# Splitting k on all 128 partitions and moving it within SBUF, and one product on GpSimd, in an attention, MoE and MLP kernel

## The chip, the cores and the metric

The kernel runs on one core of a Trainium2 chip, in one launch. The metric is the device time of an execution in microseconds (us), where less is better. Three executions of the kernel before took 638.43, 638.69 and 638.76 us; the median is 638.69. One more execution was recorded by the profiler: it took 637.58 us, of which the span of recorded instructions is 635.9. All durations below come from that one.

## The reference

Three layers follow one another, all in fp32: windowed attention, a mixture of four experts in which every expert is applied to every token with a weight, and an MLP with a squared ReLU.

```python
def _attn_ref(q, k, v):                      # B, H, S, D = 2, 8, 576, 64
    scores = 1 / sqrt(D) * np.matmul(q, k.transpose(0, 1, 3, 2))
    rel = pos[:, None] - pos[None, :]
    bias = slopes[:, None, None] * (-np.abs(rel))[None]
    mask = (rel >= 0) & (rel < 128)
    scores = np.where(mask, scores + bias[None], -1e9)
    attn = np.exp(scores - scores.max(-1, keepdims=True))
    return np.matmul(attn / (attn.sum(-1, keepdims=True) + 1e-9), v)

def _moe_ref(x, domain_probs, w1, w2):       # N, D, E, F = 1152, 512, 4, 1024
    p = domain_probs / (domain_probs.sum(-1, keepdims=True) + 1e-9)
    for e in range(E):
        out += p[:, e:e + 1] * (np.maximum(x @ w1[e], 0.0) @ w2[e])

def _moe2_ref(x, w_in, w_out):               # 512 -> 2048 -> 512
    h = np.maximum(x @ w_in, 0.0)
    return h * h @ w_out
```

## The kernel before

TensorE multiplies in the number format fp32r, which holds fewer bits than fp32. So an operand is split in two: a high part, which is the value rounded to fp32r (`rounded`, lines L555 on ACT and L557 on DVE), and a low part, which is what the rounding left (`rest`, L561, on DVE or POOL). A product is then high by high, low by high and high by low.

The attention is cut into 20 units. A unit is two heads of one batch and some queries with the keys in their windows. Units 0 to 3 are the first query tile and take q and k unsplit. Units 4 to 11 hold 256 queries and 384 keys each, units 12 to 19 hold 192 queries and 320 keys. A unit of the later sixteen has these steps, named as in the code: `lq`, `lk`, `lv` load q (L699, two DMAs in units 12 to 19), k (L706) and v (L714; L719 and L720 too in units 12 to 19), all on SP's queue; `qh`, `kh` round q and k; `ql`, `kl` take the rests; the scores on PE (L922, L931); the join with the mask (L949) and the row maximum (L969) on DVE; the exponential on ACT (L979); the division by the row sum (`no`, L1002 on ACT or L1008 on POOL); the transpose of the probabilities on PE (`tp`, L1018); masks on POOL (L1039); the product with v on PE (`pv`, L812), whose result is again rounded (xh) and its rest taken (xl).

Scores need k in a tile `khl` of 128 partitions by 2 heads by keys: the high part of both heads on partitions 0 to 63, the low part on partitions 64 to 127. q is laid out twice over the partitions, so one matmul of 128 rows does two of the three products. The load of k puts both heads beside each other on 64 partitions (`rk`, 64x2x384 or 64x2x320), so `kh` and `kl` of a unit are one instruction each on 64 partitions with 768 or 640 columns.

While attention runs, PE also does the first items of the first expert: the first products (`hps`, L1103) and the second (`yacc`, L1343). A class `Plan` puts the steps of units and items in one order before anything is emitted. Each step states which engines can do it, how long it holds the engine and when its result is there (numbers written in the code), what it depends on, which buffer slots it takes (`SLOTS`) and a due time. The planner takes, again and again, the engine that can start soonest, and on it the step that is due first. The order in which steps are taken is the order of the instructions on each engine's queue, which runs strictly in order. So costs and due times in the code set the order, and what is late on the chip waits in that order.

The weights of the experts are multiplied by the router's probabilities of a token, divided by their sum: `norm_probs` does this on all 1152 tokens at once, on DVE (a sum L1086, a reciprocal L1087 and a product L1088 on the 128x9x4 tile `pt`). Its first reader is the evacuation of the first expert's output (L1359, `y<-yacc,pt`). The name `pt` is also that of the transposed attention probabilities, which are other tiles.

From 120 us on the kernel is experts and MLP alone, where the change touches nothing.

Of the kernel before, what the change touches and what calls it, by code (L numbers as in the profile page):

```python
# [8 lines left out]
F32 = mybir.dt.float32  # L9
F32R = mybir.dt.float32r  # L10
# [6 lines left out]
P = 128  # L17
# [31 lines left out]
class Plan:  # L49
# [21 lines left out]
    def add(  # L71
        self, name, opts, fn, deps=(), takes=(), bufs=(), due=0.0, follow=(), cold=True,
        shared=False
    ):
        t = dict(
            name=name, opts=opts, fn=fn, deps=[d for d in deps if d], takes=list(takes),
            bufs=list(takes) + list(bufs), due=due + LATER.get(name, 0.0), end=None, follow=[d for d in follow if d],
            cold=cold, shared=shared,
        )
        for b in t["bufs"]:  # L80
            b.users += 1
        self.tasks.append(t)
        return t
# [74 lines left out]
def kernel(  # L158
# [14 lines left out]
    nc = tc.nc  # L173
    B, H, _, S = qT.shape
    D = v.shape[2] // H
# [25 lines left out]
    pt = probs_sum[:, :, 0:E]  # L201
    psum_p = const.tile([P, NTILE], F32, name="psum_p")

    def f32(ap):
        return ap.bitcast(F32)
# [318 lines left out]
    def where(key, u, opts):  # L524
# [1 line left out]
        return [x for x in opts if x[0] == ENGINE.get((key, u), x[0])]  # L526

    SLOTS = dict(
        rq=3, rk=2, rv=4, qh=2, ql=2, khl=2, sc=2, rsc=2, tp=2, ts=5, st=5, pt=4, work=2, y=2, h=4
    )  # L530
    plan = Plan(SLOTS)
    actx = ExitStack()
    abias = actx.enter_context(tc.tile_pool(name="abias", bufs=1))
    asp = actx.enter_context(tc.tile_pool(name="asp", bufs=2))
    psum = dict(
        sc=[actx.enter_context(tc.tile_pool(name="psc", bufs=2, space=PSUM))],
# [13 lines left out]
    def a_tile(kind, shape, dtype):  # L550
        return asp.tile(shape, dtype, tag=kind, name=kind, bufs=SLOTS[kind])

    def rounded(eng, out, in_):
        if eng == "ACT":
            nc.scalar.activation(out=out, in_=in_, func=ACTF.Copy)  # L555
        else:
            nc.vector.tensor_copy(out=out, in_=in_)  # L557

    def rest(eng, out, in0, in1):
        e = nc.gpsimd if eng == "POOL" else nc.vector  # L560
        e.tensor_tensor(out=out, in0=in0, in1=f32(in1), op=ALU.subtract)  # L561


    def act(n):
        return ("ACT", 0.01 + 0.00098 * n, 0.11 + 0.00098 * n)

    def dve(n):
        return ("DVE", 0.07 + 0.00105 * n, 0.17 + 0.00105 * n)

    def gps(n):  # L570
        return ("POOL", 0.17 + 0.0021 * n, 0.24 + 0.0021 * n)
# [24 lines left out]

    bias = abias.tile([P, H, 2 * P], BF16, name="bias")

    rel = abias.tile([P, 2 * P], F32, name="rel")

    below = abias.tile([P, P], F32, name="below")

# [66 lines left out]
    task = {}  # L669
# [6 lines left out]
    def unit_tasks(u, due):  # L676
# [3 lines left out]
        G = 2 * nb  # L680
# [4 lines left out]


        raw = t0 == 0
        b_ = {k: Buf(k) for k in ("rq", "rk", "rv", "qh", "ql", "khl", "pt", "work")}
        prev = {"pv": task.get(("pv", u - 1)) or task.get(("pv", u - 2))}

        def add(key, opts, fn, **kw):
            task[key, u] = plan.add(f"{key}{u}", opts, fn, **kw)
            return task[key, u]
# [8 lines left out]
                )  # L702

        def load_k(eng):
            t = b_["rk"].tile = a_tile("rk", [D, G, nk], F32)
            nc.sync.dma_start(  # L706
                out=t, in_=kT[bs[0], 2 * c:2 * c + 2, :, k0:q1].rearrange("a p s -> p a s")
            )
# [25 lines left out]


        def kh(eng):
            b_["khl"].tile = a_tile("khl", [P, G, nk], F32R)
            rounded(eng, b_["khl"].tile[0:D], b_["rk"].tile)

        def kl(eng):  # L740
            t = b_["khl"].tile
            rest(eng, t[D:P], b_["rk"].tile, t[0:D])

        end = due[-1]
        first = due[0]
# [11 lines left out]
        if not raw:  # L757
            tqh = add("qh", [act(G * nq), dve(G * nq)], qh, shared=True, deps=[lq], takes=[b_["qh"]],
                      bufs=[b_["rq"]], due=first - 9.0)
            tkh = add("kh", [act(G * nk), dve(G * nk)], kh, shared=True, deps=[lk], takes=[b_["khl"]],  # L760
                      bufs=[b_["rk"]], due=first - 9.1)
            tql = add("ql", [gps(G * nq), dve(G * nq)], ql, shared=True, deps=[tqh], takes=[b_["ql"]],
                      bufs=[b_["rq"], b_["qh"]], due=first - 8.2)
            tkl = add("kl", [dve(G * nk), gps(G * nk)], kl, shared=True, deps=[tkh],
                      bufs=[b_["rk"], b_["khl"]], due=first - 8.3)

        split = []
        wide = 0
# [2 lines left out]
        pos = 0  # L771
        for i, t in enumerate(range(t0, t1)):
            split += job_tasks(
                u, i, t, add, b_, due[i], loads if raw else [tqh, tql, tkh, tkl], G, q0, k0,
                pos, wide,
            )
            pos += tile_n(t) * (1 if t == 0 else 2)
# [307 lines left out]
    def norm_probs(eng):  # L1085
        nc.vector.tensor_reduce(out=psum_p, in_=probs_sum, axis=mybir.AxisListType.X, op=ALU.add)  # L1086
        nc.vector.reciprocal(out=psum_p, in_=psum_p)  # L1087
        nc.vector.tensor_tensor(  # L1088
            out=pt, in0=pt, in1=psum_p.unsqueeze(2).to_broadcast([P, NTILE, E]), op=ALU.mult
        )  # L1090


    ytile = {}

# [882 lines left out]
    t_pt = plan.add("pt", [("SP", 0.6, 6.0)], lambda eng: nc.sync.dma_start(  # L1977
        out=pt, in_=probs.rearrange("(t p) e -> p t e", p=P)
    ), deps=[wtask["load", 3]], due=50.0)
    t_np = plan.add("np", [("DVE", 0.9, 1.0)], norm_probs, deps=[t_pt], due=60.0)  # L1980
    for i in parted[:PER - (RAW1 + RAW2) // FTQ]:
        weight_parts(i)
    after = [item_tasks(it) for it in range(FT)]
# [108 lines left out]
```

## Time and profile before

| | us |
|---|---|
| median of three executions | 638.69 |
| profiled execution | 637.58 |
| its span of instructions | 635.9 |
| PE busy in the span | 630.1 (99%) |
| DVE, ACT, POOL busy | 473.5, 301.5, 377.5 |

The span and 1.68 us around it make up the profiled execution. The median of the others lies 1.11 us above it. The granted TensorE clock is full (1.00, 2.4 GHz) in every slice after the start. A matmul's records overlap, since matmuls are pipelined: what one costs is the distance to the start of the next. On SP the records are the issues of DMAs: what one costs the queue is again the distance to the next start, and the data land later.

### The profile page before, as it was taken

To read this page: it belongs to the slowest core of one execution; us is meant where nothing else is said; L and a number is where in the kernel's file an instruction comes from. 1 tells how busy PE (TensorE), PEld (TensorE's weight loads), DVE (VectorE), ACT (ScalarE), POOL (GpSimd) and SP (SyncE) were. 2 spreads that over 40 slices of the span, in tenths; PEclk is the share of its full clock that TensorE was granted. 3 is DMA by queue.
4 is the path that set the end of the run, shared out by engine and by line. 5 is a ranking of instruction groups with operands and counts; after the bars stand their busy time and mean duration, and the time that the engine had idled before them with its cause. 6 is when DMAs were issued, how large, how long until landed. Compare 5 with 4: busy or idle time off the path is not lost.

```text
span 635.9 us, 11035 instructions
## 1 busy us (share of the span) xinstructions
PE 630.1 (99%) x3918; PEld 565.0 (89%) x3918; DVE 473.5 (74%) x1027; ACT 301.5 (47%) x769; POOL 377.5 (59%) x487
## 2 busy tenths in 40 slices
PE   9999999999999999999999999999999999999997
PEld 7788889899998998998998998999999898998996
DVE  7899876388887777777777777668768767667463
ACT  8889866145444344334334444354554544343220
POOL 3597853089676446446447546246687776766531
PEclk9999999999999999999999999999999999999999
DMA  8953430222134434434434433311123223001012
GB/s 245 278 150 85 119 90 18 100 66 100 35 116 136 140 107 152 133 103 157 135 103 147 133 120 125 106 64 68 34 76 125 88 78 116 18 2 51 1 66 84
DMA packets 46983, 64.70 MB, mean 102 GB/s; under 512 B 6480, under 2 KB 29264, under 8 KB 46928
## 3 DMA queue, kind: packets, MB, share of 16 engines
q1 hardware_dynamic: 35520, 39.48, 20.2%
q10 hardware_dynamic: 11408, 24.51, 12.4%
q8 instruction: 31, 0.51, 0.3%
q14 instruction: 24, 0.20, 0.1%
HBM read 53.23 MB, written 10.75 MB: 101 GB/s over the span
## 4 chain that ended last, share of the span: by engine, by line
PE 96%; ACT 2%; DVE 1%; issue 0%; POOL 0%; POOLq 0%
PE yacc L1317 38%; PE hps L1223 35%; PE hps L1103 6%; PE yacc L1343 6%; PE xps L812 2%; PE sc L931 1%; PE tp L1018 1%; PE hps L1901 1%; PE yacc L1852 1%; ACT ts L979 1%; PE pad L588 1%; PE xtp L1409 1%; PE sc L922 1%; ACT wh L555 0%; PE xps L798 0%; ACT ts L1002 0%
## 5 line engine op out<-in xcount | busy, mean ns | idle before, releaser
L1317 PE MATMUL yacc<-wh,hmem 128*128 128x512 f32 x716 | 227.8, 390 | 0.0
L1317 PEld LDWEIGHTS yacc<-wh,hmem 128*128 128x128 f32 x716 | 134.5, 188 | 27.0
L1317 PE MATMUL yacc<-wl,hmem 128*128 128x512 f32 x358 | 139.7, 390 | 0.0
L561 POOL TENSOR_TENSOR wl<-wraw,wh 128x256 fp32r<-128x256 f32 (+1 forms) x80 | 77.0, 987 | 42.0 <-ACT wh L484 27.7
L561 POOL TENSOR_TENSOR hmem<-c,hmem 128x320 fp32r<-128x320 f32 (+1 forms) x64 | 59.2, 944 | 59.3 <-ACT hmem L1254 53.2
L561 POOL TENSOR_TENSOR ls<-wsum,hs 128x256 fp32r<-128x256 f32 x77 | 61.7, 828 | 54.3 <-ACT hs L429 53.6
L1234 ACT ACTIVATE p<-hps 128x256 f32<-128x256 f32 (+1 forms) x80 | 32.9, 411 | 108.2 <-PE hps L1223 108.1
L1238 DVE TENSOR_TENSOR u<-hps,p 128x256 f32<-128x256 f32 (+1 forms) x80 | 36.5, 456 | 64.0 <-PE hps L1223 61.7
L1317 PEld LDWEIGHTS yacc<-wl,hmem 128*128 128x128 f32 x358 | 67.3, 188 | 12.6
L561 POOL TENSOR_TENSOR la<-wraw,ha 128x256 fp32r<-128x256 f32 x54 | 49.0, 928 | 17.3 <-ACT ha L415 17.3
L322 DVE SCALAR_TENSOR_TENSOR wconv<-wraw,wconv 128x512 int32<-128x512 int32 x64 | 58.0, 906 | 1.3
L1258 ACT ACTIVATE hmem<-c 128x256 fp32r<-128x256 f32 (+1 forms) x72 | 31.2, 446 | 53.0 <-DVE c L1238 51.4
L1259 DVE SCALAR_TENSOR_TENSOR hmem<-c,hmem 128x256 fp32r<-128x256 f32 (+1 forms) x72 | 42.8, 615 | 14.2 <-ACT hmem L1258 13.2
L1254 ACT ACTIVATE hmem<-c 128x320 fp32r<-128x320 f32 (+1 forms) x64 | 27.3, 446 | 52.2 <-DVE c L1248 33.5
L405 POOL TENSOR_TENSOR wsum<-wraw 128x256 f32<-128x256 f32 x37 | 31.0, 837 | 22.0 <-PE hps L1103 14.4
L1343 PE MATMUL yacc<-wh,hmem 128*128 128x512 f32 x128 | 43.4, 395 | 0.0
L1363 DVE SCALAR_TENSOR_TENSOR y<-yacc,pt,y 128x512 f32<-128x512 f32 x54 | 37.2, 738 | 0.3 <-PE yacc L1317 0.3
L302 ACT ACTIVATE wconv<-wraw 128x512 f32<-128x512 f32 x32 | 21.4, 670 | 30.8 <-DVE wconv L322 27.6
L1223 PE MATMUL hps<-ht,ls 128*128 128x320 f32 (+1 forms) x160 | 34.4, 297 | 0.4 <-POOL ls L561 0.4
L1039 POOL TENSOR_SCALAR_AFFINE_SELECT pt<-pt 128x256 f32<-128x256 f32 (+1 forms) x64 | 28.5, 454 | 10.5 <-ACT pt L555 6.6
L1103 PE MATMUL hps<-xh,wh 128*128 128x256 f32 (+1 forms) x112 | 34.6, 309 | 0.0
L1223 PE MATMUL hps<-xh,hs 128*128 128x320 f32 (+1 forms) x160 | 34.6, 297 | 0.0
(163 smaller groups left out, 1555.9 us busy)
## 6 DMA issues: line engine op xcount, KB each, us to landing
wraw<-in_w_dram SPq DMA_DIRECT2D x32, 512.0 KB, 3.7
wraw<-in_w_out_dram ACTq DMA_DIRECT2D x16, 512.0 KB, 3.9
w<-wconv ACTq DMA_DIRECT2D x32, 256.0 KB, 3.9
wraw<-w SPq DMA_DIRECT2D x16, 512.0 KB, 3.2
wraw<-in_w_in_dram ACTq DMA_DIRECT2D x14, 512.0 KB, 3.7
rq<-in_qT_dram SPq DMA_DIRECT2D x8, 256.0 KB, 7.8
out_dram<-y SPq DMA_DIRECT2D x7, 256.0 KB, 2.1
rk<-in_kT_dram SPq DMA_DIRECT2D x8, 192.0 KB, 5.5
```

What stands on the lines that cost most here:

```text
L322: nc.vector.scalar_tensor_tensor(out=ai, in0=raw[j][:, :, part], scalar=amount, in1=ai, op0=op, op1=ALU.bitwise_or,)
L405: e_.tensor_tensor(out=t["s"][:, o:o + 2, :], in0=x(), in1=y(), op=op)
L561: e.tensor_tensor(out=out, in0=in0, in1=f32(in1), op=ALU.subtract)
L1103: nc.tensor.matmul(out=ps, lhsT=l_[:, k, cs], rhs=r_[:, k, cols], start=(k == 0 and r_ is xh and l_ is wh and not second), stop=(k == KT - ...
L1223: nc.tensor.matmul(out=ps, lhsT=a[l_][:, k, :], rhs=b[r_][:, k, :], start=start and (k, l_, r_) == (0, 0, 0), stop=stop and (k, l_) == (1, ...
L1234: nc.scalar.activation(out=out, in_=x, func=ACTF.Copy)
L1238: nc.vector.tensor_tensor(out=out, in0=x, in1=y, op=ALU.add)
L1258: nc.scalar.activation(out=hh, in_=src, func=ACTF.Relu)
L1259: nc.vector.scalar_tensor_tensor(out=hl, in0=src, scalar=0.0, in1=f32(hh), op0=ALU.max, op1=ALU.subtract)
L1317: nc.tensor.matmul(out=y, lhsT=l_[:, ns], rhs=r_[:, fo, cols], start=(first and fo == 0 and j == 0), stop=(last and fo == FTQ - 1 and j == 2),
L1343: nc.tensor.matmul(out=y, lhsT=l_[:, ns], rhs=r_[:, fo, :], start=(first and j == 0), stop=(last and j == 2),)
L1363: nc.vector.scalar_tensor_tensor(out=yt, in0=y, scalar=pt[:, nt, e:e + 1], in1=yt, op0=ALU.mult, op1=ALU.add)
```

## The change

From unit 9 on (`spread`; units 9 to 11 with 384 keys, 12 to 19 with 320), k is loaded with one head on partitions 0 to 63 and the other on 64 to 127 (`rk` 128x384 or 128x320). `kh` and `kl` work on all 128 partitions with half the columns, into a new tile `kk` of 128 partitions by 2 parts by keys, which has two slots (the tile `rel` of the start uses one of them). A new step `mk` moves the four quarters of `kk` to their places in `khl`: four DMAs from SBUF to SBUF on SP's queue, each of 64 partitions by 384 or 320 columns. Scores no longer depend on `kl` but on `mk`, which the planner books with 1.8 us of SP and 4.2 us to the result. `kh` and `kl` of these units are due 3.0 us sooner. The product of `norm_probs` becomes a step of its own on POOL.

```diff
-        rq=3, rk=2, rv=4, qh=2, ql=2, khl=2, sc=2, rsc=2, tp=2, ts=5, st=5, pt=4, work=2, y=2, h=4
+        rq=3, rk=2, rv=4, qh=2, ql=2, khl=2, kk=2, sc=2, rsc=2, tp=2, ts=5, st=5, pt=4, work=2, y=2, h=4
...
+        spread = u >= 9
...
         def load_k(eng):
+            if spread:
+                t = b_["rk"].tile = a_tile("rk", [P, nk], F32)
+                both = kT[bs[0], 2 * c:2 * c + 2, :, k0:q1]
+                nc.sync.dma_start(out=t, in_=both.rearrange("a p s -> (a p) s"))
+                return
...
         def kh(eng):
+            if spread:
+                b_["kk"].tile = a_tile("kk", [P, 2, nk], F32R)
+                rounded(eng, b_["kk"].tile[:, 0, :], b_["rk"].tile)
+                return
...
         def kl(eng):
+            if spread:
+                t = b_["kk"].tile
+                rest(eng, t[:, 1, :], b_["rk"].tile, t[:, 0, :])
+                return
...
+        def spread_k(eng):
+            t = b_["khl"].tile = a_tile("khl", [P, G, nk], F32R)
+            for x in range(2):
+                for a in range(G):
+                    nc.sync.dma_start(
+                        out=f32(t[x * D:(x + 1) * D, a, :]),
+                        in_=f32(b_["kk"].tile[a * D:(a + 1) * D, x, :]),
+                    )
...
+            m = nk * (1 if spread else G)
+            ahead = 3.0 if spread else 0.0
+            tkh = add("kh", [act(m), dve(m)], kh, shared=True, deps=[lk],
+                      takes=[b_["kk" if spread else "khl"]], bufs=[b_["rk"]],
+                      due=first - 9.1 - ahead)
...
+            if spread:
+                tkl = add("mk", [("SP", 1.8, 4.2)], spread_k, deps=[tkl], takes=[b_["khl"]],
+                          bufs=[b_["kk"]], due=first - 10.8, follow=[task.get(("mk", u - 1))])
...
     def norm_probs(eng):
         nc.vector.tensor_reduce(out=psum_p, in_=probs_sum, axis=mybir.AxisListType.X, op=ALU.add)
         nc.vector.reciprocal(out=psum_p, in_=psum_p)
-        nc.vector.tensor_tensor(
+
+
+    def share_probs(eng):
+        nc.gpsimd.tensor_tensor(
             out=pt, in0=pt, in1=psum_p.unsqueeze(2).to_broadcast([P, NTILE, E]), op=ALU.mult
         )
...
-    t_np = plan.add("np", [("DVE", 0.9, 1.0)], norm_probs, deps=[t_pt], due=60.0)
+    t_np = plan.add("np", [("DVE", 0.42, 0.5)], norm_probs, deps=[t_pt], due=59.0)
+    t_np = plan.add("sp", [("POOL", 0.3, 0.35)], share_probs, deps=[t_np], due=60.0)
```

The planner gives other orders for it. Three places matter below. The first is SP's queue between the loads of v of unit 15 and the load of k of unit 17. Before, six DMAs stand there:

```order
L714 DMA rv<-in_v_dram 128x2x128
L719 DMA rv<-in_v_dram 64x128
L720 DMA rv<-in_v_dram 64x128
L706 DMA rk<-in_kT_dram 64x2x320
L699 DMA rq<-in_qT_dram 128x2x128
L699 DMA rq<-in_qT_dram 128x2x64
```

Now there are fourteen, of which eight move k of units 15 and 16:

```order
L720 DMA rv<-in_v_dram 128x2x128
L725 DMA rv<-in_v_dram 64x128
L726 DMA rv<-in_v_dram 64x128
L762 DMA khl<-kk 64x320 x8
L700 DMA rq<-in_qT_dram 128x2x128
L700 DMA rq<-in_qT_dram 128x2x64
L709 DMA rk<-in_kT_dram 128x320
```

The loads of q and k of unit 17 are now behind those eight, and k is loaded after q instead of before it.

The second place is PE's queue between the second products of item 14 and the first products of item 15. Before (khl_1290 is k of unit 15, xps_1379 the output of unit 13, tp_1403 the transposes of unit 14):

```order
L931 MATMUL sc_163<-khl_1290,qh_1305 128x256
L931 MATMUL sc_163<-khl_1290,ql_1317 128x256
L931 MATMUL sc_163<-khl_1290,qh_1305 128x256
L931 MATMUL sc_163<-khl_1290,ql_1317 128x256
L812 MATMUL xps_1379<-pt_1256,rv_1118 64x128 x2
L812 MATMUL xps_1379<-pt_1256,rv_1118 64x192 x2
L812 MATMUL xps_1379<-pt_1256,rv_1118 64x64 x2
L812 MATMUL xps_1379<-pt_1296,rv_1139 64x128 x2
L812 MATMUL xps_1379<-pt_1296,rv_1139 64x192 x2
L812 MATMUL xps_1379<-pt_1296,rv_1139 64x64 x2
L1018 MATMUL tp_1403<-ident_80,ts_1345 128x128 x2
```

Now (the same tiles have the numbers 1361, 1399 and 1423):

```order
L841 MATMUL xps_1399<-pt_1302,rv_1159 64x128 x2
L841 MATMUL xps_1399<-pt_1302,rv_1159 64x192 x2
L841 MATMUL xps_1399<-pt_1302,rv_1159 64x64 x2
L841 MATMUL xps_1399<-pt_1337,rv_1179 64x128 x2
L841 MATMUL xps_1399<-pt_1337,rv_1179 64x192 x2
L841 MATMUL xps_1399<-pt_1337,rv_1179 64x64 x2
L1047 MATMUL tp_1423<-ident_80,ts_1382 128x128 x2
L960 MATMUL sc_163<-khl_1361,qh_1310 128x256
L960 MATMUL sc_163<-khl_1361,ql_1340 128x256
L960 MATMUL sc_163<-khl_1361,qh_1310 128x256
L960 MATMUL sc_163<-khl_1361,ql_1340 128x256
```

The scores of unit 15 have moved behind the output of unit 13 and the transposes of unit 14. In the same way the first transposes of unit 15 now stand behind the first scores of unit 16, where before they stood one item ahead of them.

The third place is ACT's queue at the rounding of k of unit 17. Before:

```order
L555 ACTIVATE khl<-rk 64x640
L555 ACTIVATE pt<-tp 128x2x64
L555 ACTIVATE qh<-rq 128x384
L979 ACTIVATE ts,st_100<-ts,st_100 128x128
L555 ACTIVATE pt<-tp 128x2x128
L1002 ACTIVATE ts<-ts,st_100 128x128
```

Now:

```order
L555 ACTIVATE kk<-rk 128x320
L555 ACTIVATE pt<-tp 128x2x64
L555 ACTIVATE qh<-rq 128x384
L1008 ACTIVATE ts,st_100<-ts,st_100 128x128
L1031 ACTIVATE ts<-ts,st_99 128x128 x2
L1964 ACTIVATE hmem<-hps 128x256
```

The rounding of k and q of unit 17 still has behind it the exponential of the unit whose softmax is under way (now unit 15), and now the division of its first tile, two instructions, is behind it as well.

## Rows read from the trace of the kernel before

**Rows 1.** Page: busy time of each engine in the span, share, instructions.

```profile
PE 630.1 (99%) x3918; PEld 565.0 (89%) x3918; DVE 473.5 (74%) x1027; ACT 301.5 (47%) x769; POOL 377.5 (59%) x487
```

**Rows 2.** Page: the chain that ended last, share of the span by engine.

```profile
PE 96%; ACT 2%; DVE 1%; issue 0%; POOL 0%; POOLq 0%
```

**Rows 3.** Windows: length, busy PE, PEld, DVE, ACT, POOL, clock, DMA share, GB/s.

```profile
50.00:60.00 10.00, 9.30 (x67) 8.30 (x66) 9.54 (x35) 8.52 (x30) 7.13 (x9) 1.00 0.36 96
60.00:120.00 60.00, 60.00 (x485) 53.34 (x484) 42.06 (x166) 38.14 (x126) 33.22 (x69) 1.00 0.27 74
```

**Rows 4.** Waits of PE: total us, times, longest.

```profile
PE hps L1103 <- DVE xl L561: 0.6, 1, 0.6
```

**Rows 5.** Timeline of DVE: start, duration, engine, line, operation.

```profile
49.30 1.09 DVE L1088 TENSOR_TENSOR pt<-pt,psum_p 128x36 f32<-128x36 f32 x1
...
51.88 0.69 DVE L561 TENSOR_TENSOR xl<-xps,xh 128x512 fp32r<-128x512 f32 x1
...
62.07 1.41 DVE L1359 TENSOR_SCALAR y<-yacc,pt 128x512 f32<-128x512 f32 x2
```

**Rows 6.** Groups on ACT, 36 to 112 us: busy us, mean ns, idle before.

```profile
L979 ACT ACTIVATE ts<-ts,st 128x128 f32<-128x128 f32 x44 | 17.3, 395 | 4.7 <-DVE st L969 4.2 <-DVE st L962 0.2
...
L1002 ACT ACTIVATE ts<-ts,st 128x128 f32<-128x128 f32 x23 | 8.0, 394 | 1.8 <-DVE st L990 1.3 <-DVE st L986 0.3
...
L555 ACT ACTIVATE khl<-rk 64x640 fp32r<-64x640 f32 x7 | 5.1, 735 | 0.7 <-PE sc L922 0.5
L555 ACT ACTIVATE qh<-rq 128x384 fp32r<-128x384 f32 x8 | 4.1, 512 | 0.0
...
L555 ACT ACTIVATE pt<-tp 128x128 f32<-128x128 f32 x6 | 1.6, 271 | 2.5 <-PE tp L1018 2.5
```

**Rows 7.** Line L561 on DVE, 36 to 112 us: ns least, median, most.

```profile
L561 DVE TENSOR_TENSOR khl<-rk,khl x11: 818/951/1589, 40.1 to 102.0; 64x640 fp32r<-64x640 f32 x7, 64x768 fp32r<-64x768 f32 x4
```

**Rows 8.** Timeline of SP's queue: DMA issues.

```profile
73.64 0.55 SPq L714 DMA_DIRECT2D rv<-in_v_dram  x1
74.24 0.50 SPq L719 DMA_DIRECT2D rv<-in_v_dram  x1
74.79 0.59 SPq L720 DMA_DIRECT2D rv<-in_v_dram  x1
75.47 1.62 SPq L714 DMA_DIRECT2D rv<-in_v_dram  x1
...
79.06 2.08 SPq L699 DMA_DIRECT2D rq<-in_qT_dram  x4
...
92.68 0.37 SPq L714 DMA_DIRECT2D rv<-in_v_dram  x1
93.11 1.50 SPq L719 DMA_DIRECT2D rv<-in_v_dram  x1
```

**Rows 9.** Timeline of SP's queue at the end: DMAs that read SBUF.

```profile
628.39 0.59 SPq L1372 DMA_DIRECT2D out_dram<-y  x1
```

**Rows 10.** DMA issues, 60 to 120 us: count, size, median us to landing.

```profile
rk<-in_kT_dram SPq DMA_DIRECT2D x6, 160.0 KB, 3.1
rq<-in_qT_dram SPq DMA_DIRECT2D x5, 128.0 KB, 2.6
rv<-in_v_dram SPq DMA_DIRECT2D x16, 32.0 KB, 2.2
```

**Rows 11.** Timeline of PE.

```profile
80.50 0.28 PE L931 MATMUL sc<-khl,qh 128*128 128x256 f32 x1
...
81.06 1.54 PE L812 MATMUL xps<-pt,rv 128*64 128x128 f32 x24
82.53 0.44 PE L1018 MATMUL tp<-ident,ts 128*128 128x128 f32 x2
82.72 0.37 PE L1103 MATMUL hps<-xh,wh 128*128 128x256 f32 x1
...
88.29 0.40 PE L1343 MATMUL yacc<-wh,hmem 128*128 128x512 f32 x1
```

More of the change, by code (lines that the diff above doesn't have):

```diff
@@ L597 @@
     bias = abias.tile([P, H, 2 * P], BF16, name="bias")
-    rel = abias.tile([P, 2 * P], F32, name="rel")
+    rel = a_tile("kk", [P, 2 * P], F32)
     below = abias.tile([P, P], F32, name="below")
@@ L687, in unit_tasks @@
         raw = t0 == 0
-        b_ = {k: Buf(k) for k in ("rq", "rk", "rv", "qh", "ql", "khl", "pt", "work")}
+        spread = u >= 9
+        b_ = {k: Buf(k) for k in ("rq", "rk", "rv", "qh", "ql", "kk", "khl", "pt", "work")}
         prev = {"pv": task.get(("pv", u - 1)) or task.get(("pv", u - 2))}
@@ L759, in unit_tasks @@
                       bufs=[b_["rq"]], due=first - 9.0)
-            tkh = add("kh", [act(G * nk), dve(G * nk)], kh, shared=True, deps=[lk], takes=[b_["khl"]],
-                      bufs=[b_["rk"]], due=first - 9.1)
+            m = nk * (1 if spread else G)
[3 more added lines that the diff above has]
+                      due=first - 9.1 - ahead)
             tql = add("ql", [gps(G * nq), dve(G * nq)], ql, shared=True, deps=[tqh], takes=[b_["ql"]],
                       bufs=[b_["rq"], b_["qh"]], due=first - 8.2)
-            tkl = add("kl", [dve(G * nk), gps(G * nk)], kl, shared=True, deps=[tkh],
-                      bufs=[b_["rk"], b_["khl"]], due=first - 8.3)
+            tkl = add("kl", [dve(m), gps(m)], kl, shared=True, deps=[tkh],
+                      bufs=[b_["rk"], b_["kk" if spread else "khl"]], due=first - 8.3 - ahead)
+            if spread:
+                tkl = add("mk", [("SP", 1.8, 4.2)], spread_k, deps=[tkl], takes=[b_["khl"]],
+                          bufs=[b_["kk"]], due=first - 10.8, follow=[task.get(("mk", u - 1))])
         split = []
@@ L773, in unit_tasks @@
             split += job_tasks(
-                u, i, t, add, b_, due[i], loads if raw else [tqh, tql, tkh, tkl], G, q0, k0,
+                u, i, t, add, b_, due[i], loads if raw else [tqh, tql, tkl], G, q0, k0,
                 pos, wide,
```

## The prediction

> **What bounds the kernel now.** I read the page's first part and then the chain of waits, to see which engine sets the end: PE is busy 99% of the span [rows 1] and holds 96% of the chain [rows 2]. The table of windows then says where it is not full. From 50 to 60 us PE is busy 9.30 of 10.00, with DVE at 9.54 and ACT at 8.52; from 60 to 120 it is busy for all 60.00, at full granted clock, with DVE at 42.06, ACT at 38.14 and POOL at 33.22 [rows 3]. So there are two kinds of place. Around 52 us PE waits for DVE, once, 0.6 us, for the rest xl [rows 4], and on DVE that rest runs at 51.88, shortly behind the product of the probabilities, 1.09 us at 49.30 [rows 5]. Behind 60 us nothing that makes DVE, ACT or POOL faster is worth anything, but whatever comes late for PE's queue is lost in full, since no idle time is left there to take it up. What the change can win is thus 0.6 us, and what it can lose is open.
>
> **The splitting of k.** How long these instructions take follows the columns, not the elements: on ACT the 64x640 rounding takes 735 ns and the 128x384 one 512, though it has more elements [rows 6]. A 128x320 rounding should take 320/384 of that, 0.43 us: 0.3 less, in each of 8 units, and some 0.3 in the three wider ones. The rests on DVE, 0.82 to 1.59 us with a median of 0.95 [rows 7], should fall by about half. Over 11 units that is 3 us of ACT and up to 5 us of DVE and POOL together. All but the units around 50 us lies beside a full PE and counts nothing.
>
> **The product on POOL.** DVE loses 1.09 us just ahead of the wait at 52 us [rows 5], so this alone could take that 0.6 us away. On POOL the product delays what is behind it by about as long; the rows show no such shape there, so I bound it by nothing and by twice 1.09. Its first reader is the evacuation at 62.07 [rows 5], over 10 us behind its place; I count 0.
>
> **The moves.** The 11 units issue 44 more DMAs on SP's queue, and the loads of later units stand behind them in strict order. What one costs the queue is the point on which all depends. Bounds: the least issue in the rows is 0.37 us, of a 128-partition load; a triple of loads of v takes from 73.64 to 75.47, 1.83 us or 0.61 each, with its 64-partition members at 0.50 and 0.59; the DMA that reads SBUF at the end takes 0.59 [rows 8, 9]. The moved pieces have 64 partitions and read SBUF, and each waits for a semaphore, so I take 0.60 from start to start, with 0.49 and 0.66 as ends. Four q loads take 2.08, 0.52 each [rows 8]; I take that for k on 128 partitions too. For the landing of a piece I take 2.2 us, that of the 32 KB loads, and for q and k 2.6 [rows 10]; SBUF to SBUF is in no row, so twice 2.2 is its upper end and half of it the lower.
>
> Now SP's queue from unit 12 on, on the clock of the trace before. The rest of k of unit 12 stands on DVE behind the two evacuations that end before at 63.4 [rows 5]; with DVE relieved by the product and three shorter rests it can end between 61 and 63.4, and I take 62.0. Only the last two pieces of that unit wait for it: 1.2, to 63.2. Load of k 14: 0.5, to 63.7. Pieces of unit 13: 2.4, to 66.1. Two triples of v: 3.7, to 69.8. Pieces of unit 14: 2.4, to 72.2. q and k of 15 and 16, six loads: 3.1, to 75.3. Two triples: 3.7, to 79.0. Pieces of unit 15: 2.4, to 81.4; the last is issued at 80.8 and landed at 83.0. From 62 to 81 us SP's queue then has no idle time.
>
> PE wants these pieces for the first scores of unit 15. In the new order they stand behind the output of unit 13 and the transposes of unit 14, so they are due where the first products of item 15 start less their own length: 82.72 less the distance 80.50 to 81.06, which is 82.16 [rows 11]. They would be 0.8 late. SP goes on: pieces of unit 16, 2.4, to 83.8; q of 17, 1.0, to 84.8; k of 17 is issued there and landed at 87.4. On ACT its rounding waits, and behind it in the queue wait the copy of transposed probabilities, the rounding of q, an exponential and two divisions of unit 15: 0.43, 0.27, 0.51, 0.40 and twice 0.39, 2.4 by the rows [rows 6], of which I take 2.2 since the records overlap. This ends at 89.6. The transposes of unit 15 wait for it. In the new order they stand behind the first scores of unit 16, so they are due at 88.29, where the next second product starts before, less their own 0.19 (82.53 to 82.72): 88.1 [rows 11]. They are 1.5 late, and that includes the 0.8, since both are read against the old clock. The load of unit 17 is late not for unit 17 but for unit 15, through ACT's order.
>
> Two issues, at 75.47 and 93.11, took 1.62 and 1.50 where their like take 0.5 [rows 8]: pauses of about 1.1. Two fall among some forty issues from 63 to 97 us; behind a queue with slack they cost nothing, in the saturated stretch they cost their length. I count half of one, 0.5. The 0.6 at 52 us gains nothing, because SP's queue and not PE's sets the time behind it.
>
> **The sum.** 637.58 of the profiled execution and 1.5 and 0.5 make 639.6. The median of the runs lies 1.11 above that execution, so the forecast is 640.7, slower by 2.0.
>
> For the ends: 18 pieces are issued from 62.0 to the deciding place (2, and four each of units 13 to 16), so 0.1 us on one moves the sum by 1.8. At 0.54 the 1.5 becomes 0.4; at 0.49 it is below zero and SP keeps up; at 0.66 it is 2.6. The end of the rest of unit 12 moves it one to one, by up to 1.0 earlier and 1.4 later.
>
> **Rival: SP keeps up (not slower).** If a piece costs 0.49 or less, 18 of them save 2.0, and nothing is late at 82 and 88 us. Then the product's 1.09 and the shorter rests of k take the 0.6 at 52 us away, and every later thing comes that much sooner: 637.58 less 0.6 is 637.0, as a median 638.1. For it speaks the 0.50 of the 64-partition loads in the triple, against it the 0.61 from start to start and the 0.59 from SBUF. It decides from 0.51 us a piece down. By its own words the Trainium skill sides with it: "DMA: Bandwidth & Descriptors", in the section "Issuing engines are not separate DMA queues", says that the sequencer's time to start a DMA is usually small relative to the DMA itself. By that rule the 44 issues would hide. The trace agrees only as far as 0.5 to 0.6 us stands against landings of 2.2 [rows 8, 10]; but issues of one queue add up where landings overlap.
>
> **Rival: the landing is slow.** If a move within SBUF takes 4.4 instead of 2.2, the scores of unit 15 come 3.0 late instead of 0.8 and take the place of the 1.5 as the latest: with the pause 637.58 and 3.5, as a median 642.2. For it speaks that 64 rows of 1280 bytes are written to 64 partitions only; against it that loads of 32 KB, in as many rows, land in 2.2 [rows 10].
>
> **Rival: pauses and longer issues together in the stretch.** 0.66 a piece and one and a half pauses: 2.6 and 1.7, as a median 643.0.
>
> **How the numbers follow.** The forecast, SP late by something like 1 to 3 us, has 0.58, with a range of its own from 639.4 to 642.0. SP keeping up has 0.26, the slow landing 0.10, the pauses 0.06. What a measurement here can tell from no change is 0.2%, or 1.28 us: below 637.41 is faster, above 639.97 slower. Of the forecast's 0.58, 0.17 lies below 639.97 (0.54 to 0.57 a piece) and 0.41 above. Slower is 0.41 and 0.10 and 0.06, 0.57; the same is 0.17 and 0.21 of the first rival, 0.38; faster 0.05, its remainder, if DVE's relief also shortens the stretch before 60 us, where PE lacks 0.7 [rows 3]. The range of 637.9 to 642.8 leaves out about half of the first rival's chance and the far part of the others.
>
> **What the new profile would show.** Right: SP's records without gaps from about 62 to 85 us, pieces at 0.55 to 0.65 from start to start; a wait of PE for the pieces before the scores of unit 15, and one for ACT's division before the transposes of unit 15, together 1 to 3 us in the 80s; the rounding of k of unit 17 on ACT waiting for its load; the 0.6 before xl gone; roundings of 128x320 at 0.43. Wrong: pieces under 0.5 and gaps on SP, with no new wait of PE; a piece's landing far over 2.2; a wait for the product on POOL at the evacuation; or a loss that lies behind 120 us, where the order of instructions is the same.

## The result and the profile after

The changed kernel takes 642.19 us (median of six runs, 641.26 to 643.25), the kernel before 638.51 in the same comparisons (637.88 to 638.76): a ratio of 1.0058, with a 95% interval of 1.0048 to 1.0069. It is slower by 3.7 us. The forecast was 640.7, slower by 2.0, with a range up to 642.8.

The profiled execution took 642.91 us, 5.33 more than that of before. Its page and its windows answer to [rows 1 to 3] (columns as there; the last three windows are where the granted clock is low):

```profile
PE 632.6 (99%) x3918; PEld 566.2 (88%) x3918; DVE 468.6 (73%) x1027; ACT 296.1 (46%) x761; POOL 376.5 (59%) x495
...
PE 89%; DMA 4%; DVE 3%; SPq 1%; ACT 1%; issue 1%; POOL 0%; ACTq 0%; DVEq 0%
```

```profile
50.00:60.00 10.00, 9.65 (x68) 8.62 (x68) 8.61 (x25) 9.26 (x29) 9.21 (x11) 1.00 0.79 204
60.00:120.00 60.00, 57.10 (x440) 49.65 (x439) 38.30 (x174) 33.47 (x122) 30.34 (x74) 0.97 0.43 107
82.00:83.00 1.00, 1.00 (x6) 0.83 (x6) 0.72 (x6) 0.88 (x5) 0.46 (x2) 0.97 0.27 74
83.00:84.00 1.00, 1.00 (x5) 0.35 (x5) 0.92 (x7) 0.69 (x4) 0.12 (x1) 0.50 0.53 120
...
86.00:87.00 1.00, 1.00 (x13) 0.85 (x10) 0.00 (x0) 0.41 (x2) 0.00 (x0) 0.83 0.48 108
```

DVE and ACT are relieved by 5 us each, and PE gains 0.35 us of work between 50 and 60. Between 60 and 120, where it had no idle time, it now loses 2.90. DMA and SP's queue have come onto the chain. From about 82.9 to 86.3 us, 3.4 us, the granted clock is at the lower of its two levels, 1.2 GHz instead of 2.4, so PE does 1.7 us less work there than at the full clock. Another 0.65 is lost before 25 us (PE's transposes stand at 23.52 before and 24.17 now), where profiles differ by themselves: in the profile of experiment 7, whose code is that of before up to unit 9, these transposes stand at 24.41. The profile of before was early there, which fits its lying 1.11 under the median. These terms make 4.9 of the 5.33; 0.4 is not placed. They say where PE's time went, not yet what set the end.

PE's waits in the new profile, against [rows 4]:

```profile
PE tp L1047 <- ACT ts L1031: 3.0, 3, 1.9
```

The wait for xl is gone, and three waits of transposes for the division on ACT (L1031, before L1002) stand in the list, 0.3 of them ahead of 60 us. Where they come from is read from SP's queue, ACT and PE in turn. SP's queue from the moves of unit 12 to the load of k of unit 17, against [rows 8]:

```profile
60.13 4.01 SPq L762 DMA_DIRECT2D khl<-kk  x4
64.18 0.58 SPq L709 DMA_DIRECT2D rk<-in_kT_dram  x1
64.88 2.38 SPq L762 DMA_DIRECT2D khl<-kk  x4
...
70.98 2.45 SPq L762 DMA_DIRECT2D khl<-kk  x4
...
76.14 0.47 SPq L709 DMA_DIRECT2D rk<-in_kT_dram  x1
76.71 0.38 SPq L720 DMA_DIRECT2D rv<-in_v_dram  x1
77.13 2.31 SPq L725 DMA_DIRECT2D rv<-in_v_dram  x1
...
81.98 5.01 SPq L762 DMA_DIRECT2D khl<-kk  x8
...
88.21 0.47 SPq L709 DMA_DIRECT2D rk<-in_kT_dram  x1
```

Four pieces take 2.4 to 2.5 us, 0.61 to 0.63 each. The first group holds the queue for 4.01, because its last two pieces wait for the rest of k of unit 12. The load of k of unit 17 is issued at 88.21. That of unit 16 is issued at 76.14, and what is issued around it lands late (DMA issues between 76 and 78.5: count, KB, us to landing):

```profile
rk<-in_kT_dram SPq DMA_DIRECT2D x1, 160.0 KB, 4.2
rv<-in_v_dram SPq DMA_DIRECT2D x1, 128.0 KB, 4.1
```

On ACT's timeline the rounding of k of unit 16 waits 1.27 for it, and the division, which needs nothing of it, stands behind:

```profile
80.53 0.47 ACT L555 ACTIVATE kk<-rk 128x320 fp32r<-128x320 f32 x1 [1.27 <-DMA rk<-in_kT_dram]
80.91 0.51 ACT L555 ACTIVATE qh<-rq 128x384 fp32r<-128x384 f32 x1
81.32 0.39 ACT L1031 ACTIVATE ts<-ts,st 128x128 f32<-128x128 f32 x1
...
91.65 0.47 ACT L555 ACTIVATE kk<-rk 128x320 fp32r<-128x320 f32 x1 [1.65 <-DMA rk<-in_kT_dram]
```

On PE the transpose waits 1.90 for that division; afterwards the clock is low, and the 24 matmuls of unit 13's output, from 81.06 to 82.53 before [rows 11], take 2.71 us to the next start:

```profile
81.76 0.33 PE L1047 MATMUL tp<-ident,ts 128*128 128x128 f32 x1 [1.90 <-ACT ts L1031]
...
83.76 2.77 PE L841 MATMUL xps<-pt,rv 128*64 128x128 f32 x24
86.47 0.44 PE L1047 MATMUL tp<-ident,ts 128*128 128x128 f32 x2
...
93.43 0.62 PE L1047 MATMUL tp<-ident,ts 128*128 128x128 f32 x2 [0.76 <-ACT ts L1031]
```

The same happens once more with k of unit 17: its rounding waits 1.65 at 91.65, and PE 0.76 at 93.43, at the transposes of unit 15.

This second place sets the end. From 64.18 to the load of k of unit 17 at 88.21 no two issues on SP lie more than 0.12 us apart, so no wait for PE held that load up. The profile's chain that ended last goes from it straight to the transposes (start, us, what):

```profile
88.21 3.34 DMA rk<-in_kT_dram
...
91.65 0.09 ACT kk L555
...
93.08 0.30 ACT ts L1031
...
93.43 0.62 PE tp L1047 x2
```

The matmuls at the low clock, from 82.9 to 86.3, are not on this chain. PE waits 0.76 at 93.43 although it lost the 1.9 and the 1.7 before; without those losses it would, by these rows, have waited there longer and not ended sooner. The forecast reads 88.1 for these transposes in the kernel before, so they are 5.3 late, as much as the two profiled executions differ.

### The profile page after: what moved, and what is told of

Read it like the earlier page. It is cut to its first block, busy times and chain, and to the rows that moved or that the text cites. A ratio compares the mean times of both kernels' runs of the same rounds, so it can differ in the third digit from the quotient of the medians.

```text
span 641.2 us, 11129 instructions
## 1 busy us (share of the span) xinstructions
PE 632.6 (99%) x3918; PEld 566.2 (88%) x3918; DVE 468.6 (73%) x1027; ACT 296.1 (46%) x761; POOL 376.5 (59%) x495
## 4 chain that ended last, share of the span: by engine, by line
PE 89%; DMA 4%; DVE 3%; SPq 1%; ACT 1%; issue 1%; POOL 0%; ACTq 0%; DVEq 0%
PE yacc L1348 38%; PE hps L1254 35%; PE yacc L1374 5%; PE hps L1134 5%; DMA rk<-in_kT_dram 3%; PE hps L1932 1%; PE xps L841 1%; PE sc L960 1%; PE yacc L1883 1%; PE tp L1047 1%; SPq L762 1%; DVE wl L561 1%; PE xtp L1440 1%; DMA rq<-in_qT_dram 1%; SPq L700 0%
## 5 line engine op out<-in xcount | busy, mean ns | idle before, releaser
L561 POOL TENSOR_TENSOR wl<-wraw,wh 128x256 fp32r<-128x256 f32 (+1 forms) x80 | 75.6, 970 | 40.0 <-ACT wh L484 27.7
L561 POOL TENSOR_TENSOR hmem<-c,hmem 128x320 fp32r<-128x320 f32 (+1 forms) x64 | 59.2, 943 | 59.4 <-ACT hmem L1285 53.4
L561 POOL TENSOR_TENSOR ls<-wsum,hs 128x256 fp32r<-128x256 f32 x77 | 61.6, 827 | 54.3 <-ACT hs L429 53.6
L561 POOL TENSOR_TENSOR la<-wraw,ha 128x256 fp32r<-128x256 f32 x54 | 48.6, 919 | 16.8 <-ACT ha L415 16.8
L1254 PE MATMUL hps<-ht,hs 128*128 128x320 f32 (+1 forms) x160 | 34.5, 297 | 0.0
```

Of the source, the lines that this page charges most:

```text
L1254: nc.tensor.matmul(out=ps, lhsT=a[l_][:, k, :], rhs=b[r_][:, k, :], start=start and (k, l_, r_) == (0, 0, 0), stop=stop and (k, l_) == (1, ...
```

## The experiments

The theory: the moves fill SP's queue, the loads of k behind them come late, and the rounding that waits for such a load holds up the softmax behind it on ACT. The rivals are the product's new place, the landing or the bytes of the moves, and the new path of k as such.

| | edit | median us | of before | ratio, 95% interval |
|---|---|---|---|---|
| 1 | the product alone | 637.81 | 638.43 | 0.9981 to 0.9999 |
| 2 | the path of k alone | 643.07 | 638.43 | 1.0065 to 1.0089 |
| 3 | pieces halved | 666.08 | 638.43 | 1.0422 to 1.0449 |
| 4 | loads of v on ACT's queue | 641.65 | 638.43 | 1.0042 to 1.0075 |
| 5 | moves on GpSimd's queue | 648.92 | 638.49 | 1.0147 to 1.0175 |
| 6 | every second unit | 641.18 | 638.49 | 1.0029 to 1.0055 |
| 7 | before with spare loads | 640.38 | 638.49 | 1.0023 to 1.0054 |
| 8 | true cost in the plan | 640.35 | 638.49 | 1.0018 to 1.0041 |
| 9 | units 9 to 11 alone | 637.66 | 638.54 | 0.9980 to 0.9999 |
| 10 | the division first | 642.56 | 638.54 | 1.0051 to 1.0076 |

**1 and 2: each part alone.** The first is the kernel before with the edits of `norm_probs`, `share_probs` and their two steps; the second is the changed kernel without them.

> The kernel before, with only the probabilities' product moved to GpSimd as a step of its own; k is loaded and split as before and nothing is moved within SBUF. Theory (the loss is SP's queue of moved pieces and ACT's order behind the late loads of k): no loss, 637.5 to 638.7 us against about 638.5 of before, the 0.6 us wait of PE for xl shorter or gone. Rival (the product on GpSimd, or the order that the planner makes with it, is what costs): 640 us or more, with a wait of PE for POOL or for the evacuation.

> The changed kernel with the product back on DVE, so that only the path of k is new. Theory (SP's queue): the loss stays, 641 to 644 us, with PE's wait for the division on ACT behind a late rounding of k between 78 and 95 us. Rival (the product's place costs): back within 1 us of before, 638 to 639.5.

```diff
-        nc.vector.tensor_tensor(
+    def share_probs(eng):
+        nc.gpsimd.tensor_tensor(
```

The product alone gains 0.6 us; on GpSimd it took 1.02 us in this run, at 50.2, over 10 us ahead of its reader. In its profile the wait for xl is gone, but one of the same 0.6 for hmem on DVE stands at 57.1 in its place, and PE is busy 9.26 of the ten, not more than before. So the gain of the medians is not that wait's, and its profile does not show where it lies; behind 60 us PE is full as before:

```profile
PE hps L1106 <- DVE hmem L1939: 0.6, 1, 0.6
```
```profile
50.00:60.00 10.00, 9.26 (x70) 8.56 (x69) 9.68 (x35) 9.28 (x31) 9.59 (x13) 1.00 0.38 100
60.00:120.00 60.00, 60.00 (x484) 53.33 (x483) 42.62 (x166) 38.82 (x131) 30.50 (x61) 1.00 0.27 74
```

The path of k alone loses 4.6, in a profile whose granted clock is 1.00 all the way: from 60 to 120 us PE is busy 56.38 of 60. So the whole loss is the path of k's, and it needs no lower clock. PE waits 0.97 for a division on ACT at 81.42, as expected, but longer for divisions on GpSimd. They follow exponentials that stand on ACT behind the rounding of q, and that waits for a late load of q:

```profile
91.65 0.53 ACT L555 ACTIVATE qh<-rq 128x384 fp32r<-128x384 f32 x1 [3.62 <-DMA rq<-in_qT_dram]
```
```profile
94.46 1.02 PE L1047 MATMUL tp<-ident,ts 128*128 128x128 f32 x3 [2.06 <-POOL ts L1037]
```

So the load can be one of q as well, and the step that PE lacks need not be on ACT itself.

**3: pieces halved.** Eight DMAs a unit of half the columns, the same bytes.

> The changed kernel with each moved piece cut in two halves of columns: 8 DMAs of 64 partitions a unit instead of 4, the same bytes, the same order. Theory (each issue holds SP's queue 0.6 us): up to the load of k of unit 16 there are some 14 issues more behind unit 12, 0.5 to 0.6 each, so 7 to 9 us later at the first stall and some more behind it: 648 to 656 us. Rival (the bytes moved or their landing decide, not the issue): as the changed kernel, 641 to 643.5.

```diff
+                    for h in (slice(0, nk // 2), slice(nk // 2, nk)):
```

27.7 us slower, far beyond the upper end of 656. The rival that the bytes or their landing decide is out: a half lands in 1.9 us, no later than a whole piece (2.1), but takes as long to issue, 0.63 from start to start. The theory had the direction and not the size: I had counted only the first stall, and nothing for the granted clock, whose mean from 60 to 120 us is 0.91. PE now waits in four places for divisions (9.3 us) and, which the changed kernel does not show, for the moves themselves:

```profile
PE tp L1048 <- ACT ts L1032: 9.3, 4, 3.8
PE sc L961 <- DMA khl<-kk: 4.8, 5, 1.6
```
```profile
72.80 4.94 SPq L763 DMA_DIRECT2D khl<-kk  x8
77.84 0.53 SPq L720 DMA_DIRECT2D rv<-in_v_dram  x1
```
```profile
khl<-kk SPq DMA_DIRECT2D x52, 40.0 KB, 1.9
```

**4: loads of v on ACT's queue.** For units 12 to 19 the three loads are issued by ACT.

> The changed kernel with the loads of v of units 12 to 19 (three DMAs each) issued from ACT's queue instead of SP's; the moves and all else stay. Theory (SP's queue is full between 62 and 90 us): two triples, 3.7 us, go from in front of the load of k of unit 16 and one or two more from in front of that of unit 17, so the load of k 16 is issued at about 72.5 instead of 76.1 and PE's waits of 3 us go or fall under 0.6: 638 to 639.8 us, ACT's 24 more issues of some 0.5 us lying in its idle time. Rival (the late thing is DVE's split or the landing of the moves, not SP's queue): 641 us or more, with the same waits. A second way to lose: ACT is held up by the issues, then the waits of PE stay but name exponentials.

```diff
+            queue = nc.scalar if u >= 12 else nc.sync
```

Nearly as slow as the changed kernel, and inconclusive, since the edit brought a delay of its own. SP's queue did not run ahead: the moves of unit 14 now waited in it for their split, and the load of k of unit 16 was issued at 75.50. ACT was held by its own issues just there: one took 1.44 us at 79.25, and ACT stood idle for 2.39 before the evacuation behind it. PE then waited 2.58 us for a division, and the granted clock stayed at 1.00:

```profile
80.74 0.38 ACT L1965 ACTIVATE hmem<-hps 128x256 fp32r<-128x256 f32 x1 [2.39 <-DMA rv<-in_v_dram]
```
```profile
82.89 0.33 PE L1048 MATMUL tp<-ident,ts 128*128 128x128 f32 x1 [2.58 <-ACT ts L1032]
```

**5: moves on GpSimd's queue.**

> The changed kernel with the 44 moves issued from GpSimd's queue instead of SP's, in the same order of steps. Theory (the moves hold SP's queue, and the loads of k behind them come late): the load of k of unit 16 is issued near 71 us instead of 76 and PE's waits behind 60 us fall under 1 us: 638 to 639.8 us, if an issue on GpSimd takes no more than on SP. No run shows that yet; at 1 us and more each the waits turn up behind GpSimd's masks instead, and the time is 640 or more with another engine named. Rival (the moves' landing, or the bytes, make the scores late): as the changed kernel, 641 to 643, with the waits at the same places.

```diff
-                    nc.sync.dma_start(
+                    nc.gpsimd.dma_start(
```

The worst place short of halving, and 9 us above the 639.8 that I expected for issues no longer than SP's: they are not longer, four take GpSimd 2.1 us, but its in-order queue holds masks and divisions behind the moves. GpSimd is busy 46.38 of 60 us (before 33.22 [rows 3]), of which 17.3 are issues, and PE waits for it:

```profile
PE tp L1047 <- POOL ts L1037: 5.2, 4, 2.4
PE xps L841 <- POOL pt L1068: 2.5, 2, 1.8
```

That the issues cost time wherever they are made agrees with the theory; whether SP alone would have been early enough, this run can't tell.

**6: every second unit.** The new path in units 10, 12, 14, 16 and 18 only.

> The changed kernel with the new path of k in units 10, 12, 14, 16 and 18 only, 20 moves instead of 44. Theory (SP's queue, 0.6 us a piece): ahead of the load of k of unit 16 stand 4 pieces less behind unit 12's, of unit 17 8 less: 2.4 and 5 us earlier, so PE waits under 1 us behind 60 us and the time is 637.6 to 639.5. Rival (any use of the new path costs, by the landing of a unit's own moves): 639.5 to 641, the loss about halved.

```diff
-        spread = u >= 9
+        spread = u >= 9 and u % 2 == 0
```

2.7 us slower: with 20 moves instead of 44, two thirds of the loss stay, against my 637.6 to 639.5. The planner has made another order for it: the load of k of unit 16 stands behind three loads of v, is issued at 76.78, later than in the changed kernel, and lands 3.7 later; its rounding waits 2.37 us on ACT. PE then waits for steps of GpSimd that come after steps of ACT behind that rounding, a mask and a division:

```profile
80.62 0.47 ACT L555 ACTIVATE kk<-rk 128x320 fp32r<-128x320 f32 x1 [2.37 <-DMA rk<-in_kT_dram]
```
```profile
82.17 0.66 PE L841 MATMUL xps<-pt,rv 128*64 128x192 f32 x8 [0.52 <-POOL pt L1068]
83.87 0.68 PE L1047 MATMUL tp<-ident,ts 128*128 128x128 f32 x2 [1.04 <-POOL ts L1037]
```

So the loss does not count moves. It asks when the one load arrives behind which ACT holds a softmax.

**7: the kernel before with spare loads.** Four loads of 64 partitions more behind each load of k from unit 9 on, into a tile without a reader.

> The kernel before, with four more DMAs of 64 partitions by half a unit's keys behind each load of k from unit 9 on, into a tile that nobody reads: 44 issues more on SP, without a wait for an engine's work, without moves within SBUF. Theory (the issues by themselves fill SP's queue): the load of k of unit 17 comes some 16 to 20 issues later, 8 to 11 us against a slack of about 1, less what SP's idle time before 64 us takes up: 642 to 650 us. Rival (what costs is that a move waits in the queue for the split of k, or its landing): these loads wait for nothing, 638 to 640.

```diff
+            if u >= 9:
+                spare = a_tile("spare", [D, 4, nk // 2], F32)
+                for x in range(4):
+                    h = k0 + (x // 2) * (nk // 2)
+                    nc.sync.dma_start(
+                        out=spare[:, x, :], in_=kT[bs[0], 2 * c + x % 2, :, h:h + nk // 2]
+                    )
```

1.9 us slower, between the two expectations. The issues alone do delay: the load of k of unit 17, at 78.35 before, is issued here at 85.89, 7.5 later against the 8 to 11 reckoned. But PE does not wait for that one; it loses 1.6 us (busy 58.41 of 60) by the load of k of unit 16, issued at 79.02 instead of 72.91 and landed 3.0 later, as before. Its rounding begins at 82.11, behind it on ACT stands the copy of transposed probabilities, behind that a mask on GpSimd:

```profile
82.11 0.74 ACT L555 ACTIVATE khl<-rk 64x640 fp32r<-64x640 f32 x1 [1.80 <-PE sc L938]
```
```profile
84.26 0.66 PE L819 MATMUL xps<-pt,rv 128*64 128x192 f32 x8 [1.17 <-POOL pt L1046]
```

(The profile puts ACT's wait down to scores on PE, which end at the same time as that landing.) So extra issues, in the order of before and without a move, make the same kind of stall, and about half of the loss. These loads read HBM, which the moves do not; that k of unit 16 still lands in 3.0 speaks against their bytes. The other half lies in what the change brings beside it: another order, and moves that wait in the queue for their split. This run does not part these two; experiment 8 changes the order alone.

**8: the true cost in the plan.** The planner books 2.5 us of SP and 4.7 to the result.

> The changed kernel with the planner's cost of the moves at 2.5 us of SP and 4.7 to the result instead of 1.8 and 4.2, so that its order allows for what an issue takes. Theory (the order was made for a queue that is faster than the chip's): the planner puts less in front of late things, PE waits fall by about half, 638.8 to 641 us. Rival (SP has too much to do in any order): 641 to 643.5.

```diff
-                tkl = add("mk", [("SP", 1.8, 4.2)], spread_k, ...
+                tkl = add("mk", [("SP", 2.5, 4.7)], spread_k, ...
```

The loss is halved, to 1.9, with the same 44 moves: the two waits of 1.9 and 0.76 are gone, and PE is busy 58.93 of 60. So half of the loss goes with the order that the planner made for a queue faster than the chip's. That the truer costs, and not just any other order, bring this is not shown by one such order; the orders of experiments 6 and 10 left more.

**9: units 9 to 11 alone.** Twelve moves; the last eight are issued from 51.6 to 56.7 us.

> The changed kernel with the new path of k in units 9, 10 and 11 only: 12 moves, all issued before about 62 us, and the product on GpSimd. Theory (what costs is SP's queue behind 62 us; what helps is the relief of DVE and ACT from 50 to 60 us): the waits behind 60 us are gone, PE is busy 9.6 or more of the 10 us from 50 to 60, 637.3 to 638.3 us, as good as the product alone (637.81) or a little better. Rival (the new path costs by itself, wherever it is used): 639 us or more.

```diff
-        spread = u >= 9
+        spread = 9 <= u < 12
```

0.9 us faster than before by the medians, and within 0.2 of the product alone, from which it is not told apart here. The new path by itself costs nothing where SP has time; PE has 0.35 more from 50 to 60 and is full behind 60 us:

```profile
50.00:60.00 10.00, 9.65 (x69) 8.58 (x68) 8.61 (x25) 8.61 (x28) 9.50 (x11) 1.00 0.77 187
60.00:120.00 60.00, 59.96 (x485) 53.20 (x484) 40.33 (x173) 36.99 (x128) 34.19 (x72) 1.00 0.28 76
```

**10: the division first.** One more dependency for the rounding of k of units 16 and 17.

> The changed kernel with one more dependency in the plan: the rounding of k of unit 16 comes after the division of unit 13's last tile, that of unit 17 after the division of unit 15's first. SP's queue stays as it is up to the moves of unit 15. Theory (PE's 1.9 us wait at 81.8 is the division standing behind the rounding of k 16 on ACT, which waits for the late load): this wait falls under 0.5, and part of it comes back when unit 16's scores wait for their later moves: 639.3 to 641.3 us. Rival (PE would have waited there anyway, for the scores or their softmax): the waits stay at 2.5 to 3 us, 641.5 to 643.

```diff
+            early = {16: ("j1no", 13), 17: ("j0no", 15)}.get(u)
...
-            tkh = add("kh", [act(m), dve(m)], kh, shared=True, deps=[lk],
+            tkh = add("kh", [act(m), dve(m)], kh, shared=True,
+                      deps=[lk] + ([task[early]] if early else []),
```

The load of k of unit 16 is issued at 76.16 and lands 4.2 later, as in the changed kernel. The division now stands ahead of its rounding, and the wait of 1.9 has become 0.39:

```profile
79.76 0.40 ACT L1033 ACTIVATE ts<-ts,st 128x128 f32<-128x128 f32 x1
80.45 0.47 ACT L555 ACTIVATE kk<-rk 128x320 fp32r<-128x320 f32 x1 [0.30 <-DMA rk<-in_kT_dram]
```
```profile
80.21 0.33 PE L1049 MATMUL tp<-ident,ts 128*128 128x128 f32 x1 [0.39 <-ACT ts L1033]
```

That shows the link from the late load through ACT's order to PE. But the time is 642.56, above my 639.3 to 641.3, and PE's waits behind 60 us are again 3.0 in all: the numbers are the rival's, at another place. What was won at 82 us is lost again from 95 on, where PE is busy 3.19 of 5 us. The load of k of unit 18 is issued at 91.05 (in the changed kernel at 91.52), its rounding waits 3.47 for it, and behind that stands the copy for which GpSimd's mask and then PE wait:

```profile
94.54 0.47 ACT L555 ACTIVATE kk<-rk 128x320 fp32r<-128x320 f32 x1 [3.47 <-DMA rk<-in_kT_dram]
```
```profile
96.33 0.44 PE L843 MATMUL xps<-pt,rv 128*64 128x128 f32 x4 [0.78 <-POOL pt L1070]
```

Where SP's queue is behind, mending one stall moves it to the next: PE, no longer held up at 82, comes sooner to the work behind the next load, and that load hardly sooner (0.5 us).

## Why the prediction was right, step by step

**The mechanism held.** That PE is full from 60 us on and so loses every late thing, that the relief is worth 0.6 at most, that 44 issues of about 0.6 fill SP's queue, and that the time is lost through ACT's order, with a division of an older unit behind the rounding of a newer unit's k: all of it stands in the new profile. Experiments 1 and 9 show that neither the product nor the new path where SP has time is the loss, 3 and 7 that issues by themselves bring it, and 10 that the way from a late load to PE leads through ACT's order. What the prediction had too narrow: in experiments 2, 6 and 7 PE waits for GpSimd, one step behind ACT. The pieces take 0.61 to 0.63 for the 0.60 of the sum, their landing is 2.1 us for 2.2 (the rival of a slow landing is out), the roundings take 470 ns for 430, the product 0.70 on GpSimd, far ahead of its reader.

**The size was low: 2.0 for 3.7.** The 642.19 lies inside the whole range, 0.2 above the 642.0 at which the forecast's own ended. The place that sets the end is the one named, the transposes of unit 15 behind the rounding of k of unit 17. But they are 5.3 late where the sum had 1.5 and 0.5, because that load is issued at 88.21 and not at 84.8 and lands later. The terms:

First, the rest of k of unit 12 was to end at 62.0. It ended at 63.0, 1.0 later. It took 1.21 us where others on DVE took 0.49; GpSimd was at work beside it, but that this is the reason is not shown. Up to 0.65 of the 1.0 may be the later start of this execution.

```profile
61.80 1.21 DVE L561 TENSOR_TENSOR kk<-rk,kk 128x320 fp32r<-128x320 f32 x1
```

Second, the pause, of which I counted half of one, is not a matter of chance. It comes in at least nine of the twelve profiles between 75 and 81 us, with whatever DMA stands there: in the product alone at 76.12 with 1.46, in the changed kernel at 77.13 with 2.31, in experiment 6 at 77.46 with 2.02, before at 75.47 with 1.62 [rows 8]. So it falls into the full stretch, and is 1.8 above an issue of 0.5 where I took 0.5. All the other issues up to 88.21 are together 0.6 longer than reckoned.

Third, the landing of the load of k that decides was to be 2.6 and was 3.3; from there to the end of the division ACT took 1.8 instead of 2.2. With 1.0, 1.8, 0.6 and 0.7 more and 0.4 less the 1.5 becomes 5.2.

The medians are only 3.7 apart, since the profiled execution of before lies 1.11 under its median and that of the changed kernel 0.72 above its own; the sum took the 1.11 for both. So it is by luck that terms 3.3 short miss the median by only 1.5.

Two things are not in the sum. One is a first stall, a unit earlier than I looked: the division of unit 13 behind the rounding of k of unit 16, 1.9 us at 81.76. Its load landed 4.2 after its issue, where I took 2.6; it was under way in the pause, and while the 16 DMA engines were busy for 0.84 of the time from 76 to 78 us, and no run parts the two. By this stall and the low clock PE came to unit 15's scores, the first place that I had named, only at 86.66. Their last piece was issued at 83.84, so with 2.1 to land it was there, and they did not wait. The stall did not set the end, as the chain shows; experiment 10 took it away and won nothing.

The other is the granted clock. Of the six runs of the changed kernel, two have a mean clock of 1.0 over the whole span and took 641.26 and 641.77 us; the four at 0.996 to 0.997 took 642.14 to 643.25. By these medians, 641.5 and 642.6, a low clock goes with some 1.1 us. That it costs them is not shown: it is off the chain in this kernel's one profile, and neither of the two runs at 1.0 was profiled. Nor is a long wait enough to bring it: in experiment 4 PE waited 2.58 us and in experiment 2 2.06, more than the 1.9 here, and the clock stayed at 1.00.

**The rival of a slow landing** had 642.2, the measured time, by chance: the moves land in 2.1, not in 4.4.

**The rival that SP keeps up** failed: the pieces cost 0.61 to 0.63, above the 0.51 from which it decides. The rule of the Trainium skill that I set beside it ("DMA: Bandwidth & Descriptors", "Issuing engines are not separate DMA queues": starting a DMA is usually a small time against the DMA itself) fits the single DMA here, 0.6 against 2.1 to land, but does not carry over to the queue, where 28 pieces between 60 and 100 us add up to 17 us of SP, while their landings overlap.

## What to carry to other kernels

Work that is split over more partitions and then moved back is paid for by issues on an in-order queue: count them in us, add the wait of a move for its producer, and look at which loads stand behind. The harm comes out elsewhere, where an engine keeps a finished unit's work behind the first touch of a later unit's load; mending that order alone moves the stall on. Use such a path where the queue is idle (units 9 to 11 here), and tell a planner what an issue really takes (experiment 8, one order).

## What the runs showed that was not expected

Where an issue on SP takes 1 to 2.3 us instead of 0.5, the DMA queue named instruction has a packet in the same 2 us, and loads then under way land late, in up to 4.2 us. This is that queue's row in the changed kernel from 76 to 78 us (packets, MB, share of 16 engines' time):

```profile
q8 instruction: 1, 0.02, 5.3%
```

There is one in the kernel before as well, from 74 to 76 and again from 92 to 94 us, and its two long issues stand at 75.47 and 93.11 [rows 8]. Where the attention runs later, the pair does too: in experiment 3 a long issue at 83.31 with such a packet between 81 and 85, in experiment 5 one at 85.35 with one between 85 and 90. Such packets come every 14 to 20 us from 60 us on, in both kernels; those at 60 and 106 before meet no issue on SP. That the one makes the other is only argued; no run took such a packet away.

The product of 128x9x4 takes 1.09 us on DVE [rows 5] and 0.70 to 1.02 on GpSimd.
